# Splitting a 2048-point sequence transform as 128 × 16 with a radix-8 instead of a radix-4 vector stage

## The chip, the cores and the metric

The kernel runs on one core of a Trainium2 chip. The metric is the device time of one execution in microseconds (us). The kernel before took 253.74 us in the median of six runs (253.08 to 256.08).

The engines go by the names the profile gives them: PE multiplies matrices (PEld is its weight load, which overlaps the multiplications), DVE is the vector engine, ACT the scalar engine, POOL and SP here mostly issue DMA transfers. Each engine works through its own instruction list in order.

## The reference, cut to what matters

```python
xn = _layernorm(x, axis=-1)                       # x: 1 x 2048 x 512, bf16
return x + _A_ref(xn, w_r, w_i) + _B_ref(xn, w_gate, w_up, w_down)

def _A_ref(x, w_r, w_i):                          # spectral branch
    X = jnp.fft.rfft2(x.astype(jnp.float32), axes=(-2, -1))
    X = X * (w_r + 1j * w_i)                      # w_r, w_i: 2048 x 257
    return jnp.fft.irfft2(X, s=(S, D), axes=(-2, -1)).astype(jnp.bfloat16)

def _B_ref(x, w_gate, w_up, w_down):              # gated branch
    g = x @ w_gate; u = x @ w_up                  # 512 -> 1792
    return (_gelu(g) * u) @ w_down                # 1792 -> 512
```

S is 2048 (the sequence axis) and D is 512 (the feature axis). A real transform of 512 points has 257 distinct complex outputs, which is where the width of 257 in the kernel comes from.

## The kernel before

Everything is unrolled into straight lists of instructions, one list per engine. A scheduler writes these lists when the kernel is built: of the instructions whose inputs and buffers are free by its own estimate of times, it takes the one with the highest priority. Priority is the order in the program, so the gated branch (lines 265 to 311) comes ahead of the spectral branch; only instructions inside `with hp():` are lifted ahead of everything. Those are matmuls and ACT copies of the spectral branch (lines 327 to 336, 351 to 367 and 431 to 456). The spectral branch's DVE work is not lifted.

**Normalization (lines 232 to 260).** x lies in 16 blocks of 128 rows, where block `b = 8*T + rho` holds the rows `1024*T + 8*tau + rho`. Each block is normalized on DVE, transposed on PE and copied by ACT to `xnT`.

**Gated branch.** There are four chunks of 512 rows, and in each chunk 14 tiles of the hidden axis, 56 tiles in all. For one tile PE runs four `gps` and four `ups` matmuls of 512 columns (lines 271 and 277). ACT and DVE then make the GELU: ACT `sq` and `gsb` from PSUM (283, 285), DVE `wtl` and `z` (287, 292), ACT `sg` (294), DVE `m1` and the product with `ups` into `hT` (296, 297). After the 14 tiles of a chunk, four `dn` accumulations of 14 matmuls each (303) give the branch's output rows; DVE adds x to each and keeps it as `bsp` (310). The tiles `sq`, `gsb`, `wtl`, `z`, `sg` and `m1` come from a pool with two buffers each, so the chain of one tile can overlap that of the next. PSUM has two buffers for `gps`, three for `ups` and one for `dn`.

**Spectral branch, forward.** The feature axis is transformed by matmuls with a cosine and sine matrix `Gt` (`pd`, lines 330 to 335), and ACT copies the result to `Pt`. The sequence axis of 2048 points is then split. With k = 512*m + 128*kc + i, the loop over four `kc` (line 339) loads one 1 MB table `Fkc` and two 257 KB pieces of the spectral weights. For each of four residues r, eight matmuls sum four blocks each against cosine and sine (`cs`, lines 354 and 362). ACT copies them out in four pieces, and DVE combines the halves to `qq` (368, 370). A 4-point transform over r on DVE (`bf`, then `XFk`, lines 373 to 389) gives four values of m, which are multiplied by the complex weights (`tm`, lines 396 to 401).

**Spectral branch, inverse.** After two values of `kc` that belong together (q = kc mod 2), the function `dft8` (line 125) runs an 8-point inverse transform over the eight values of m on DVE and writes `YY`; lines 413 to 421 negate and patch its edges. When both halves q of `YY` are there, 128 `ut` matmuls of 256 columns (line 451) with the 2 MB table `Rt` and 64 `fp` matmuls of 512 columns (468) return to the sequence and feature axes. DVE adds `bsp` (472) and two 1 MB transfers write the output.

Of the kernel before, what the change touches and what calls it, by code (L numbers as in the profile page):

```python
# [12 lines left out]
BF16 = mybir.dt.bfloat16  # L13
ALU = mybir.AluOpType
# [3 lines left out]
D = 512  # L18
DF = 1792
P = 128  # L20
# [4 lines left out]
def _host_constants():  # L25
# [26 lines left out]
    tau = np.arange(P).astype(np.int64)  # L52
    T8 = np.arange(2).astype(np.int64)
    rho8 = np.arange(8).astype(np.int64)
    mp = np.arange(P).astype(np.int64)
    kcv = np.arange(4).astype(np.int64)
    s_val = (1024 * T8[:, None, None] + 8 * tau[None, :, None] + rho8[None, None, :])
    sv = s_val.transpose(1, 0, 2)
    prod = (128 * kcv[:, None, None, None, None] + mp[None, None, None, None, :]) * sv[None, :, :, :, None]
    angF = 2.0 * np.pi * (prod % S) / S  # L60
    Fcos = np.cos(angF).reshape(4, P, 16, P)
    Fsin = np.sin(angF).reshape(4, P, 16, P)
    F = np.stack([Fcos, Fsin], axis=2).reshape(4, P, 2 * 16 * P)
    ii = np.arange(P).astype(np.int64)
    qv = np.arange(2).astype(np.int64)
    tp = np.arange(256).astype(np.int64)
# [6 lines left out]
    bf = ml_dtypes.bfloat16  # L73
# [10 lines left out]
def kernel(  # L84
# [24 lines left out]
    gview = cG.rearrange("(p dt) k -> p dt k", dt=4)  # L109
    giview = cGinv.rearrange("(kt p) d -> p kt d", p=P)  # L110
    rview = cR.rearrange("i (q cs r t) -> i q cs r t", q=2, cs=2, r=8)
    wrv4 = A_w_r.rearrange("(m kc i) k -> i kc m k", m=4, kc=4)
    wiv4 = A_w_i.rearrange("(m kc i) k -> i kc m k", m=4, kc=4)

    tt = nc.vector.tensor_tensor
    HP_OFF = 10_000_000
# [148 lines left out]
    for c in range(4):  # L265
        hT = hpool.tile([P, 14, D], BF16)
        for fc in range(14):
            gps = psA.tile([P, D], FP32)
            ups = psA.tile([P, D], FP32, bufs=3)
            for dt in range(4):  # L270
                nc.tensor.matmul(  # L271
                    gps[:], lhsT=wg[:, dt, fc * P:(fc + 1) * P],
                    rhs=xnT[:, dt, 4 * c:4 * c + 4, :], start=(dt == 0),
                    stop=(dt == 3),
                )
            for dt in range(4):
                nc.tensor.matmul(  # L277
                    ups[:], lhsT=wu[:, dt, fc * P:(fc + 1) * P],
                    rhs=xnT[:, dt, 4 * c:4 * c + 4, :], start=(dt == 0),
                    stop=(dt == 3),  # L280
                )
            sq = mpool.tile([P, D], BF16)
            nc.scalar.activation(out=sq[:], in_=gps[:], func=ACT.Square)  # L283
            gsb = mpool.tile([P, D], BF16)
            nc.scalar.copy(out=gsb[:], in_=gps[:])  # L285
            wtl = mpool.tile([P, D], BF16)
            nc.vector.tensor_scalar(  # L287
                out=wtl[:], in0=sq[:], scalar1=A3, scalar2=C1, op0=ALU.mult,
                op1=ALU.add,
            )  # L290
            z = mpool.tile([P, D], BF16)
            tt(out=z[:], in0=wtl[:], in1=gsb[:], op=ALU.mult)  # L292
            sg = mpool.tile([P, D], BF16)
            nc.scalar.activation(out=sg[:], in_=z[:], func=ACT.Sigmoid, scale=2.0)  # L294
            m1 = mpool.tile([P, D], BF16)
            tt(out=m1[:], in0=sg[:], in1=gsb[:], op=ALU.mult)
            tt(out=hT[:, fc, :], in0=m1[:], in1=ups[:], op=ALU.mult)  # L297
# [19 lines left out]
    with tc.tile_pool(name="p3f", bufs=1) as p3f, tc.tile_pool(  # L317
        name="p3ps", bufs=1, space=bass.MemoryType.PSUM
    ) as p3ps, tc.tile_pool(name="p3g", bufs=1) as p3g, tc.tile_pool(
        name="p3q", bufs=1  # L320
    ) as p3q, tc.tile_pool(name="p3xf", bufs=2) as p3xf, tc.tile_pool(
        name="p3w", bufs=1
    ) as p3w, tc.tile_pool(name="p3cs", bufs=1, space=bass.MemoryType.PSUM) as p3cs:
        Pt = p3f.tile([P, 16, D], BF16)
        blocks4 = [[8 * T8 + r4 + 4 * hi for T8 in range(2) for hi in range(2)]
                   for r4 in range(4)]
        with hp():
            for r4 in range(4):
                for b in blocks4[r4]:
                    pd = p3ps.tile([P, D], FP32)  # L330
                    for dt in range(4):
                        nc.tensor.matmul(  # L332
# [2 lines left out]
                        )  # L335
                    nc.scalar.copy(out=Pt[:, b, :], in_=pd[:])

        XF_by_kc = {}
        for kc in (0, 2, 1, 3):
            Fkc = p3g.tile([P, 2, 16, P], BF16)  # L340
            WRk = p3w.tile([P, 4, 258], BF16)
            WIk = p3w.tile([P, 4, 258], BF16)
            nc.sync.dma_start(
                out=Fkc[:], in_=cF[kc].rearrange("t (c b m) -> t c b m", c=2, b=16)
            )
            nc.sync.dma_start(out=WRk[:, :, 0:257], in_=wrv4[:, kc, :, :])
            nc.sync.dma_start(out=WIk[:, :, 0:257], in_=wiv4[:, kc, :, :])
            qq = p3q.tile([P, 4, 2, 258], BF16)
            for r in range(4):
                cbsb = p3q.tile([P, 2, 256], BF16, tag="cbsb", bufs=1)  # L350
                with hp():
                    cs = p3cs.tile([P, D], FP32, tag="cs")
                    for n, b in enumerate(blocks4[r]):
                        nc.tensor.matmul(  # L354
                            cs[:], lhsT=Fkc[:, 0, b, :], rhs=Pt[:, b, :],
                            start=(n == 0), stop=(n == 3),
                        )
                    nc.scalar.copy(out=qq[:, r, 0, 0:257], in_=cs[:, 0:257])
                    nc.scalar.copy(out=cbsb[:, 0, 0:255], in_=cs[:, 257:512])
                    cs2 = p3cs.tile([P, D], FP32, tag="cs")  # L360
                    for n, b in enumerate(blocks4[r]):
                        nc.tensor.matmul(
                            cs2[:], lhsT=Fkc[:, 1, b, :], rhs=Pt[:, b, :],
                            start=(n == 0), stop=(n == 3),
                        )
                    nc.scalar.copy(out=qq[:, r, 1, 0:257], in_=cs2[:, 0:257])
                    nc.scalar.copy(out=cbsb[:, 1, 0:255], in_=cs2[:, 257:512])
# [1 line left out]
                   in1=cbsb[:, 1, 0:255], op=ALU.subtract)  # L369
                tt(out=qq[:, r, 1, 1:256], in0=qq[:, r, 1, 1:256],  # L370
                   in1=cbsb[:, 0, 0:255], op=ALU.add)
            bf = p3q.tile([P, 2, 4, 258], BF16)
            for p_ in range(2):
                tt(out=bf[:, p_, 0, 0:257], in0=qq[:, 0, p_, 0:257], in1=qq[:, 2, p_, 0:257], op=ALU.add)
                tt(out=bf[:, p_, 1, 0:257], in0=qq[:, 0, p_, 0:257], in1=qq[:, 2, p_, 0:257], op=ALU.subtract)
                tt(out=bf[:, p_, 2, 0:257], in0=qq[:, 1, p_, 0:257], in1=qq[:, 3, p_, 0:257], op=ALU.add)
                tt(out=bf[:, p_, 3, 0:257], in0=qq[:, 1, p_, 0:257], in1=qq[:, 3, p_, 0:257], op=ALU.subtract)
            s02r, d02r, s13r, d13r = (bf[:, 0, k, 0:257] for k in range(4))
            s02i, d02i, s13i, d13i = (bf[:, 1, k, 0:257] for k in range(4))
            XFk = p3xf.tile([P, 4, 2, 258], BF16)  # L380
            XF_by_kc[kc] = XFk
            tt(out=XFk[:, 0, 0, 0:257], in0=s02r, in1=s13r, op=ALU.add)
            tt(out=XFk[:, 0, 1, 0:257], in0=s02i, in1=s13i, op=ALU.add)
            tt(out=XFk[:, 2, 0, 0:257], in0=s02r, in1=s13r, op=ALU.subtract)
            tt(out=XFk[:, 2, 1, 0:257], in0=s02i, in1=s13i, op=ALU.subtract)
            tt(out=XFk[:, 1, 0, 0:257], in0=d02r, in1=d13i, op=ALU.subtract)
            tt(out=XFk[:, 1, 1, 0:257], in0=d02i, in1=d13r, op=ALU.add)
            tt(out=XFk[:, 3, 0, 0:257], in0=d02r, in1=d13i, op=ALU.add)
            tt(out=XFk[:, 3, 1, 0:257], in0=d02i, in1=d13r, op=ALU.subtract)
            for m in range(4):  # L390
                tm = p3w.tile([P, 4, 258], BF16, tag="tm")
                xr_ = XFk[:, m, 0, 0:257]
                xq_ = XFk[:, m, 1, 0:257]
                w_r = WRk[:, m, 0:257]
                w_i = WIk[:, m, 0:257]
                tt(out=tm[:, 0, 0:257], in0=xr_, in1=w_r, op=ALU.mult)
                tt(out=tm[:, 1, 0:257], in0=xq_, in1=w_i, op=ALU.mult)
                tt(out=tm[:, 2, 0:257], in0=xr_, in1=w_i, op=ALU.mult)
                tt(out=tm[:, 3, 0:257], in0=xq_, in1=w_r, op=ALU.mult)
                tt(out=XFk[:, m, 0, 0:257], in0=tm[:, 0, 0:257], in1=tm[:, 1, 0:257], op=ALU.add)  # L400
                tt(out=XFk[:, m, 1, 0:257], in0=tm[:, 2, 0:257], in1=tm[:, 3, 0:257], op=ALU.subtract)
            if kc >= 2:
                q = kc - 2
                Xe, Xo = XF_by_kc[q], XF_by_kc[kc]
                ins = []
                for m8 in range(8):
                    src = Xe if m8 % 2 == 0 else Xo
                    m4 = m8 // 2
                    ins.append((src[:, m4, 0, 0:257], src[:, m4, 1, 0:257]))
                outs_ = [(YY[:, q, rp, 0, 0:257], YY[:, q, rp, 1, 0:257]) for rp in range(8)]  # L410
                dft8(ins, outs_, SC)
                for rp in range(8):
                    nc.vector.tensor_scalar(
                        out=YY[:, q, rp, 2, 0:257], in0=YY[:, q, rp, 1, 0:257],
                        scalar1=-1.0, scalar2=None, op0=ALU.mult,
                    )
                    nc.vector.tensor_copy(
                        out=YY[:, q, rp, 1, 256:257], in_=YY[:, q, rp, 0, 256:257]
                    )
                    nc.vector.tensor_copy(  # L420
                        out=YY[:, q, rp, 0, 256:257], in_=YY[:, q, rp, 2, 256:257]
                    )

    p3ut = ctx.enter_context(tc.tile_pool(name="p3ut", bufs=1))
    UT = p3ut.tile([P, 8, 4, 256], BF16)
# [78 lines left out]
```

## Time and profile before

| | us |
|---|---|
| median of six runs | 253.74 |
| the profiled execution, its own time | 254.92 |
| its span from first to last instruction | 253.1 |
| PE busy in it | 230.5 (91%) |
| DVE busy in it | 191.0 (75%) |
| ACT busy in it | 143.3 (57%) |

The mean granted PE clock is 0.993 of full speed. Two habits of the profile matter. The recorded duration of a matmul is longer than the distance between the starts of two matmuls in a row[...]: 128x512 matmuls are recorded with some 380 ns, but four of them take 0.86 us on the chain of work that ended last. DVE records overlap in the same way. What a stage can carry is therefore read from the distance of starts, and a busy share tells only whether something was in flight.

### The profile page before, as it was taken

What the parts mean: (1) busy time and instruction counts of PE and PEld (TensorE: products, weight loads), DVE (VectorE), ACT (ScalarE), POOL (GpSimd) and SP (SyncE); (2) the same over time, 40 slices, a digit from 0 to 9 for tenths busy, and PEclk for the clock granted to TensorE, in tenths of its full rate; (3) what the DMA queues carried; (4) which work ended last, traced back from release to release, by engine and by line L of the source; (5) the groups of instructions that cost most, each with busy time, mean ns of one, the idle gap of its engine ahead of it and who ended that gap; (6) DMA issues with size and microseconds to landing.
All of it is one profiled execution on the core that took longest, in us unless ns stands there. A gap on an engine that the chain in (4) does not pass through costs nothing.

```text
span 253.1 us, 3506 instructions
## 1 busy us (share of the span) xinstructions
PE 230.5 (91%) x1120; PEld 107.4 (42%) x1120; DVE 191.0 (75%) x661; ACT 143.3 (57%) x302; POOL 11.6 (5%) x20
## 2 busy tenths in 40 slices
PE   0398999999999989999999999999899999999990
PEld 0254444444444334444444443444344467644440
DVE  2997664346999989999946999999899970144571
ACT  2279987768753328986334888830269987600000
POOL 8530000000000000000000000000000000000000
PEclk9999999999999999999999999999999999999997
DMA  6999920001303503000105021009100000000044
GB/s 222 350 348 372 326 84 1 0 3 23 142 22 103 187 18 88 1 3 0 38 26 186 4 45 38 0 7 351 39 21 0 5 0 0 3 0 0 0 166 166
DMA packets 9954, 21.45 MB, mean 85 GB/s; under 512 B 785, under 2 KB 7057, under 8 KB 9041
## 3 DMA queue, kind: packets, MB, share of 16 engines
q1 hardware_dynamic: 8112, 13.12, 15.9%
q0 software_dynamic: 1824, 8.13, 9.1%
q8 instruction: 8, 0.13, 0.2%
q14 instruction: 10, 0.07, 0.1%
HBM read 19.14 MB, written 2.10 MB: 84 GB/s over the span
## 4 chain that ended last, share of the span: by engine, by line
PE 55%; DVE 24%; ACT 8%; DMA 8%; issue 3%; DVEq 0%; POOLq 0%; ACTq 0%
PE ups L277 11%; PE gps L271 10%; PE dn L303 9%; PE ut L451 6%; PE fp L468 6%; DVE hT L297 5%; PE cs L354 4%; PE pd L332 4%; DMA Rt<-cR 3%; DVE z L292 3%; DMA Fkc<-cF 2%; ACT sg L294 2%; DVE stats L242 2%; DMA xt<-in_A_x_dram 2%; ACT sq L283 2%
## 5 line engine op out<-in xcount | busy, mean ns | idle before, releaser
L271 PE MATMUL gps<-xnT,wg 128*128 128x512 bf16 x224 | 61.6, 383 | 0.1
L277 PE MATMUL ups<-xnT,wu 128*128 128x512 bf16 x224 | 61.2, 381 | 0.2 <-DVE hT L297 0.2
L303 PE MATMUL dn<-wd,hT 128*128 128x512 bf16 x224 | 53.5, 379 | 0.9 <-DVE hT L297 0.6
L283 ACT ACTIVATE sq<-gps 128x512 bf16<-128x512 f32 x56 | 33.3, 595 | 26.9 <-PE gps L271 26.5
L294 ACT ACTIVATE sg<-z 128x512 bf16<-128x512 bf16 x56 | 35.3, 632 | 15.1 <-DVE z L292 14.1
L303 PEld LDWEIGHTS <-hT 128*128 128x128 bf16 x224 | 21.8, 97 | 29.5 <-issue 2.6
L277 PEld LDWEIGHTS <-wu 128*128 128x128 bf16 x224 | 22.0, 98 | 26.4 <-issue 2.4
L285 ACT CAST gsb<-gps 128x512 bf16<-128x512 f32 x56 | 32.7, 584 | 0.0
L271 PEld LDWEIGHTS <-wg 128*128 128x128 bf16 x224 | 22.0, 99 | 24.8 <-issue 0.7
L287 DVE TENSOR_SCALAR wtl<-sq 128x512 bf16<-128x512 bf16 x56 | 16.1, 288 | 19.6 <-ACT sq L283 19.5
L292 DVE TENSOR_TENSOR z<-wtl,gsb 128x512 bf16<-128x512 bf16 x56 | 23.5, 420 | 2.5 <-ACT gsb L285 2.3
L354 PE MATMUL cs<-Pt,Fkc 128*128 128x512 bf16 x64 | 18.4, 378 | 1.4 <-DMA Fkc<-cF 1.2
L310 DVE TENSOR_TENSOR bsp<-xblk,dn 128x512 bf16<-128x512 bf16 x16 | 10.9, 684 | 10.8 <-PE dn L303 10.8
L451 PE MATMUL ut<-Rt,YY 128*128 128x256 bf16 x128 | 17.1, 271 | 1.8 <-DMA Rt<-cR 1.1
L257 PE MATMUL tp<-ident,xn 128*128 128x128 bf16 x64 | 7.9, 263 | 11.6 <-DVE xn L251 10.6
L332 PE MATMUL pd<-Gt,xnT 128*128 128x512 bf16 x64 | 16.4, 379 | 0.0
L451 PEld LDWEIGHTS <-YY 128*128 128x128 bf16 x128 | 12.1, 97 | 8.0 <-issue 3.0
L468 PE MATMUL fp<-Ginv,UT 128*128 128x512 bf16 x64 | 14.9, 378 | 0.0
L456 ACT CAST UT<-ut 128x256 bf16<-128x256 f32 x32 | 11.6, 375 | 3.7 <-PE ut L451 3.0
L472 DVE TENSOR_TENSOR osb<-bsp,fp 128x512 bf16<-128x512 bf16 x16 | 11.0, 688 | 3.3 <-PE fp L468 3.3
L242 DVE BATCH_NORM_STATS2 stats<-xt 128x6 f32<-128x512 bf16 x16 | 10.4, 663 | 4.0 <-DMA xt<-in_A_x_dram 4.0
L257 PEld LDWEIGHTS <-xn 128*128 128x128 bf16 x64 | 5.9, 128 | 15.0 <-DVE xn L251 11.3
(222 smaller groups left out, 263.5 us busy)
## 6 DMA issues: line engine op xcount, KB each, us to landing
Fkc<-cF SPq DMA_DIRECT2D x4, 1024.0 KB, 5.5
xt<-in_A_x_dram SPq DMA_DIRECT2D x4, 512.0 KB, 6.1
xblk<-in_A_x_dram SPq DMA_DIRECT2D x16, 128.0 KB, 2.6
Rt<-cR POOLq DMA_DIRECT2D x1, 2048.0 KB, 8.8
out_dram<-osb SPq DMA_DIRECT2D x2, 1024.0 KB, 3.9
wd<-in_B_w_down_dram POOLq DMA_DIRECT2D x2, 896.0 KB, 15.9
wg<-in_B_w_gate_dram POOLq DMA_DIRECT2D x4, 384.0 KB, 16.3
wu<-in_B_w_up_dram POOLq DMA_DIRECT2D x4, 384.0 KB, 16.2
```

The costliest lines, as they stand in the source:

```text
L271: nc.tensor.matmul(gps[:], lhsT=wg[:, dt, fc * P:(fc + 1) * P], rhs=xnT[:, dt, 4 * c:4 * c + 4, :], start=(dt == 0), stop=(dt == 3),)
L277: nc.tensor.matmul(ups[:], lhsT=wu[:, dt, fc * P:(fc + 1) * P], rhs=xnT[:, dt, 4 * c:4 * c + 4, :], start=(dt == 0), stop=(dt == 3),)
L283: nc.scalar.activation(out=sq[:], in_=gps[:], func=ACT.Square)
L285: nc.scalar.copy(out=gsb[:], in_=gps[:])
L287: nc.vector.tensor_scalar(out=wtl[:], in0=sq[:], scalar1=A3, scalar2=C1, op0=ALU.mult, op1=ALU.add,)
L292: tt(out=z[:], in0=wtl[:], in1=gsb[:], op=ALU.mult)
L294: nc.scalar.activation(out=sg[:], in_=z[:], func=ACT.Sigmoid, scale=2.0)
L303: nc.tensor.matmul(dn[:], lhsT=hT[:, fc, r * P:(r + 1) * P], rhs=wd[:, fc, :], start=(fc == 0), stop=(fc == 13),)
L332: nc.tensor.matmul(pd[:], lhsT=xnT[:, dt, b, :], rhs=Gt[:, dt, :], start=(dt == 0), stop=(dt == 3),)
L354: nc.tensor.matmul(cs[:], lhsT=Fkc[:, 0, b, :], rhs=Pt[:, b, :], start=(n == 0), stop=(n == 3),)
L451: nc.tensor.matmul(ut[:], lhsT=lt, rhs=rh, start=(q == 0 and pi_ == 0), stop=(q == 1 and pi_ == 1),)
L468: nc.tensor.matmul(fp[:], lhsT=UT[:, rp, t, aT * P:(aT + 1) * P], rhs=Ginv[:, t, :], start=(t == 0), stop=(t == 3),)
```

## The change

The sequence transform is split as 2 halves q times 8 values of m: k = 256*m + 128*q + i. Each half now loads one 1 MB table `Fq` and two 514 KB pieces of the weights, so two tables are loaded in place of four. For each of eight residues r, four matmuls sum two blocks each. The 4-point transform over r becomes an 8-point one, done by a first call of `dft8` into `XFq`; after the weights a second call of `dft8`, the one there was, writes `YY`. The order of the `pd` blocks follows the new residues. `qq`, `XFq` and the weight tiles have eight slots in place of four, `bf` is gone, the pool of `XFq` has one buffer in place of two, and the gated branch's `wtl`, `z` and `sg` have one buffer each in place of two.

```diff
-            wtl = mpool.tile([P, D], BF16)
+            wtl = mpool.tile([P, D], BF16, bufs=1)
...
-            z = mpool.tile([P, D], BF16)
+            z = mpool.tile([P, D], BF16, bufs=1)
...
-            sg = mpool.tile([P, D], BF16)
+            sg = mpool.tile([P, D], BF16, bufs=1)
...
-    ) as p3q, tc.tile_pool(name="p3xf", bufs=2) as p3xf, tc.tile_pool(
+    ) as p3q, tc.tile_pool(name="p3xf", bufs=1) as p3xf, tc.tile_pool(
...
-        for kc in (0, 2, 1, 3):
-            Fkc = p3g.tile([P, 2, 16, P], BF16)
-            WRk = p3w.tile([P, 4, 258], BF16)
-            WIk = p3w.tile([P, 4, 258], BF16)
+        for q in range(2):
+            Fq = p3g.tile([P, 2, 16, P], BF16)
+            WRq = p3w.tile([P, 8, 258], BF16)
+            WIq = p3w.tile([P, 8, 258], BF16)
...
-            for r in range(4):
+            for r in range(8):
...
-                    for n, b in enumerate(blocks4[r]):
+                    for T8 in range(2):
+                        b = 8 * T8 + r
                         nc.tensor.matmul(
-                            cs[:], lhsT=Fkc[:, 0, b, :], rhs=Pt[:, b, :],
-                            start=(n == 0), stop=(n == 3),
+                            cs[:], lhsT=Fq[:, 0, b, :], rhs=Pt[:, b, :],
+                            start=(T8 == 0), stop=(T8 == 1),
                         )
...
-            bf = p3q.tile([P, 2, 4, 258], BF16)
-            for p_ in range(2):
-                tt(out=bf[:, p_, 0, 0:257], in0=qq[:, 0, p_, 0:257], in1=qq[:, 2, p_, 0:257], op=ALU.add)
...
-            tt(out=XFk[:, 3, 1, 0:257], in0=d02i, in1=d13r, op=ALU.subtract)
-            for m in range(4):
+            XFq = p3xf.tile([P, 8, 2, 258], BF16)
+            dft8(
+                [(qq[:, n, 0, 0:257], qq[:, n, 1, 0:257]) for n in range(8)],
+                [(XFq[:, m, 0, 0:257], XFq[:, m, 1, 0:257]) for m in range(8)],
+                SC,
+            )
+            for m in range(8):
...
+            dft8(
+                [(XFq[:, m, 0, 0:257], XFq[:, m, 1, 0:257]) for m in range(8)],
+                [(YY[:, q, rp, 0, 0:257], YY[:, q, rp, 1, 0:257]) for rp in range(8)],
+                SC,
+            )
```

More of the change, by code (lines that the diff above doesn't have):

```diff
@@ L54, in _host_constants @@
     rho8 = np.arange(8).astype(np.int64)
-    mp = np.arange(P).astype(np.int64)
-    kcv = np.arange(4).astype(np.int64)
+    iv0 = np.arange(P).astype(np.int64)
+    qv0 = np.arange(2).astype(np.int64)
     s_val = (1024 * T8[:, None, None] + 8 * tau[None, :, None] + rho8[None, None, :])
     sv = s_val.transpose(1, 0, 2)
-    prod = (128 * kcv[:, None, None, None, None] + mp[None, None, None, None, :]) * sv[None, :, :, :, None]
+    prod = (128 * qv0[:, None, None, None, None] + iv0[None, None, None, None, :]) * sv[None, :, :, :, None]
     angF = 2.0 * np.pi * (prod % S) / S
-    Fcos = np.cos(angF).reshape(4, P, 16, P)
-    Fsin = np.sin(angF).reshape(4, P, 16, P)
-    F = np.stack([Fcos, Fsin], axis=2).reshape(4, P, 2 * 16 * P)
+    Fcos = np.cos(angF).reshape(2, P, 16, P)
+    Fsin = np.sin(angF).reshape(2, P, 16, P)
+    F = np.stack([Fcos, Fsin], axis=2).reshape(2, P, 2 * 16 * P)
     ii = np.arange(P).astype(np.int64)
@@ L111 @@
     rview = cR.rearrange("i (q cs r t) -> i q cs r t", q=2, cs=2, r=8)
-    wrv4 = A_w_r.rearrange("(m kc i) k -> i kc m k", m=4, kc=4)
-    wiv4 = A_w_i.rearrange("(m kc i) k -> i kc m k", m=4, kc=4)
+    wrv = A_w_r.rearrange("(m q i) k -> i q m k", m=8, q=2)
+    wiv = A_w_i.rearrange("(m q i) k -> i q m k", m=8, q=2)
     tt = nc.vector.tensor_tensor
@@ L324 @@
         Pt = p3f.tile([P, 16, D], BF16)
-        blocks4 = [[8 * T8 + r4 + 4 * hi for T8 in range(2) for hi in range(2)]
-                   for r4 in range(4)]
         with hp():
-            for r4 in range(4):
-                for b in blocks4[r4]:
+            for r8 in range(8):
+                for T8 in range(2):
+                    b = 8 * T8 + r8
                     pd = p3ps.tile([P, D], FP32)
@@ L336 @@
                     nc.scalar.copy(out=Pt[:, b, :], in_=pd[:])
-        XF_by_kc = {}
-        for kc in (0, 2, 1, 3):
-            Fkc = p3g.tile([P, 2, 16, P], BF16)
-            WRk = p3w.tile([P, 4, 258], BF16)
-            WIk = p3w.tile([P, 4, 258], BF16)
+        for q in range(2):
+            Fq = p3g.tile([P, 2, 16, P], BF16)
+            WRq = p3w.tile([P, 8, 258], BF16)
+            WIq = p3w.tile([P, 8, 258], BF16)
             nc.sync.dma_start(
-                out=Fkc[:], in_=cF[kc].rearrange("t (c b m) -> t c b m", c=2, b=16)
+                out=Fq[:], in_=cF[q].rearrange("t (c b m) -> t c b m", c=2, b=16)
             )
-            nc.sync.dma_start(out=WRk[:, :, 0:257], in_=wrv4[:, kc, :, :])
-            nc.sync.dma_start(out=WIk[:, :, 0:257], in_=wiv4[:, kc, :, :])
-            qq = p3q.tile([P, 4, 2, 258], BF16)
-            for r in range(4):
+            nc.sync.dma_start(out=WRq[:, :, 0:257], in_=wrv[:, q, :, :])
+            nc.sync.dma_start(out=WIq[:, :, 0:257], in_=wiv[:, q, :, :])
+            qq = p3q.tile([P, 8, 2, 258], BF16)
+            for r in range(8):
                 cbsb = p3q.tile([P, 2, 256], BF16, tag="cbsb", bufs=1)
@@ L352 @@
                     cs = p3cs.tile([P, D], FP32, tag="cs")
-                    for n, b in enumerate(blocks4[r]):
+                    for T8 in range(2):
+                        b = 8 * T8 + r
                         nc.tensor.matmul(
-                            cs[:], lhsT=Fkc[:, 0, b, :], rhs=Pt[:, b, :],
-                            start=(n == 0), stop=(n == 3),
+                            cs[:], lhsT=Fq[:, 0, b, :], rhs=Pt[:, b, :],
+                            start=(T8 == 0), stop=(T8 == 1),
                         )
@@ L360 @@
                     cs2 = p3cs.tile([P, D], FP32, tag="cs")
-                    for n, b in enumerate(blocks4[r]):
+                    for T8 in range(2):
+                        b = 8 * T8 + r
                         nc.tensor.matmul(
-                            cs2[:], lhsT=Fkc[:, 1, b, :], rhs=Pt[:, b, :],
-                            start=(n == 0), stop=(n == 3),
+                            cs2[:], lhsT=Fq[:, 1, b, :], rhs=Pt[:, b, :],
+                            start=(T8 == 0), stop=(T8 == 1),
                         )
@@ L371 @@
                    in1=cbsb[:, 0, 0:255], op=ALU.add)
-            bf = p3q.tile([P, 2, 4, 258], BF16)
-            for p_ in range(2):
-                tt(out=bf[:, p_, 0, 0:257], in0=qq[:, 0, p_, 0:257], in1=qq[:, 2, p_, 0:257], op=ALU.add)
[L375 to L388, printed above, removed]
-            tt(out=XFk[:, 3, 1, 0:257], in0=d02i, in1=d13r, op=ALU.subtract)
-            for m in range(4):
+            XFq = p3xf.tile([P, 8, 2, 258], BF16)
[5 more added lines that the diff above has]
+            for m in range(8):
                 tm = p3w.tile([P, 4, 258], BF16, tag="tm")
[L392 to L395, printed above, removed]
+                xr_ = XFq[:, m, 0, 0:257]
+                xq_ = XFq[:, m, 1, 0:257]
+                w_r = WRq[:, m, 0:257]
+                w_i = WIq[:, m, 0:257]
                 tt(out=tm[:, 0, 0:257], in0=xr_, in1=w_r, op=ALU.mult)
@@ L399 @@
                 tt(out=tm[:, 3, 0:257], in0=xq_, in1=w_r, op=ALU.mult)
[L400 to L422, printed above, removed]
+                tt(out=XFq[:, m, 0, 0:257], in0=tm[:, 0, 0:257], in1=tm[:, 1, 0:257], op=ALU.add)
+                tt(out=XFq[:, m, 1, 0:257], in0=tm[:, 2, 0:257], in1=tm[:, 3, 0:257], op=ALU.subtract)
+            dft8(
[3 more added lines that the diff above has]
+            )
+            for rp in range(8):
+                nc.vector.tensor_scalar(
+                    out=YY[:, q, rp, 2, 0:257], in0=YY[:, q, rp, 1, 0:257],
+                    scalar1=-1.0, scalar2=None, op0=ALU.mult,
+                )
+                nc.vector.tensor_copy(
+                    out=YY[:, q, rp, 1, 256:257], in_=YY[:, q, rp, 0, 256:257]
+                )
+                nc.vector.tensor_copy(
+                    out=YY[:, q, rp, 0, 256:257], in_=YY[:, q, rp, 2, 256:257]
+                )
     p3ut = ctx.enter_context(tc.tile_pool(name="p3ut", bufs=1))
```

## The prediction

> **What bounds the kernel now.** I read the page's busy table and its 40 slices first.
>
> ```profile
> PE 230.5 (91%) x1120; PEld 107.4 (42%) x1120; DVE 191.0 (75%) x661; ACT 143.3 (57%) x302; POOL 11.6 (5%) x20
> ...
> PE   0398999999999989999999999999899999999990
> ...
> DVE  2997664346999989999946999999899970144571
> ```
>
> PE looks like the bound. But DVE, 75% on the mean, shows 9s from about 60 to 200 us, so there are two bounds in that stretch. The answer by windows makes this exact; I cut at 60 us and at 206.5 us, where DVE issues the last operation on YY.
>
> ```profile
> core 0: us, PE busy (x) PEld busy (x) DVE busy (x) ACT busy (x) POOL busy (x), PEclk, DMA share, GB/s
> 15.00:60.00 45.00, 43.97 (x220) 20.40 (x219) 26.49 (x74) 36.10 (x74) 1.34 (x2) 1.00 0.43 141
> 60.00:206.50 146.50, 141.82 (x657) 63.02 (x655) 137.68 (x533) 91.02 (x194) 0.55 (x1) 1.00 0.18 58
> 206.50:253.10 46.60, 40.57 (x222) 21.20 (x220) 16.60 (x26) 10.78 (x28) 0.00 (x0) 0.96 0.11 45
> ```
>
> In the middle stretch DVE has something in flight for 137.7 of 146.5 us: whatever is added to it there moves the moment when YY is complete. I call that moment T. What follows T is the tail, from the timeline:
>
> ```profile
> 206.22 0.28 DVE L420 COPY YY<-YY 128x1 bf16<-128x1 bf16 x2
> ...
> 206.69 12.22 PE L451 MATMUL ut<-Rt,YY 128*128 128x256 bf16 x92
> 218.75 1.03 PE L271 MATMUL gps<-xnT,wg 128*128 128x512 bf16 x4
> 219.61 1.03 PE L277 MATMUL ups<-xnT,wu 128*128 128x512 bf16 x4
> 220.47 3.29 PE L303 MATMUL dn<-wd,hT 128*128 128x512 bf16 x14
> ```
>
> After T come the rest of ut, one gated tile (1.7 us), all four dn of the last chunk (12.4 us, from 3.1 each on the chain) and fp; all of it is PE work. The last fp ends at 247.4, and the last add and the output transfer take 5.7 more.
>
> Third, the timeline of a stretch dense with gated tiles, for the real price of a DVE operation and for the use of the double buffers.
>
> ```profile
> 98.65 0.29 DVE L123 TENSOR_TENSOR SC<-SC 128x257 bf16<-128x257 bf16 x1
> 98.85 0.42 DVE L292 TENSOR_TENSOR z<-wtl,gsb 128x512 bf16<-128x512 bf16 x1
> ...
> 99.52 1.36 ACT L294 ACTIVATE sg<-z 128x512 bf16<-128x512 bf16 x2
> ...
> 99.79 0.42 DVE L292 TENSOR_TENSOR z<-wtl,gsb 128x512 bf16<-128x512 bf16 x1
> ...
> 100.33 0.42 DVE L296 TENSOR_TENSOR m_756<-sg,gsb 128x512 bf16<-128x512 bf16 x1
> ```
>
> The 257-wide operation is recorded with 0.29 us, but its successor starts 0.20 us later. Starts in a row elsewhere give 0.203 for it, 0.135 for a 257-wide negation, 0.065 for a one-column copy, and 0.20, 0.335, 0.335 and 0.60 for wtl, z, m1 and hT: 1.47 us of DVE a tile; bsp is 0.60. This list can be tested: 45 tiles (66.2), 12 bsp (7.2) and the spectral operations after 60 us (65.4 of them in all, less some 2.0 before) make 136.8 us, against 137.7 measured. So DVE is costed by starts.
>
> **The change, part by part.**
>
> *PE, removed.* 4 kc x 4 r x 8 = 128 cs matmuls become 2 x 8 x 4 = 64. By 0.216 us each (0.86 for four on the chain) that is 13.8 us. The first half q has 32, as kc = 0 had, beside the same 64 pd, so nothing is gained before 60 us; the gain lies in the middle stretch. The waits for F shrink too, by 1.2 us at 89 us, where PE stood for the second table.
>
> *DVE, added.* bf and XFk go: 4 x 16 = 64 operations. Two more dft8 come, each of 52 two-operand operations and 4 scalings: 104 and 8. Net 40 x 0.203 + 8 x 0.135 = 9.2 us. Here a rule speaks against my price. The Trainium skill, "VectorE: DVE Perf Modes", section "The DRAIN you can't avoid", says that the next operation does not start until the pipe is empty (and that one not held starts earlier). By full recorded durations the sum would be 40 x 0.291 + 8 x 0.224 = 13.4 us. The rows show the next start inside the recorded duration, and the ledger closes to 1 us with starts, so I take 9.2.
>
> *ACT.* 64 copies out of cs before, 64 after; but 32 fall in the first half instead of 16 in kc = 0. Their starts are about 0.28 apart, so 4.5 us more come on ACT between 28 and 62, where it is busy some 75% of the time. This may delay a gated tile or so (1.5 us of DVE later); against it the even half of the first dft8 can start before 60, in DVE's idle time there (up to 12 operations, 2.4 us). I count -1 us for both; bounds -2.4 and +2.
>
> *Waits in the middle.* DVE's 8.7 us of idleness there are nearly all listed in its timeline. 5.5 of them lie at 127 to 135 us, when it had no spectral work and waited for cs, dn and ACT:
>
> ```profile
> 130.10 0.69 DVE L310 TENSOR_TENSOR bsp<-xblk,dn 128x512 bf16<-128x512 bf16 x1 [1.65 <-PE dn L303]
> ...
> 134.93 0.29 DVE L370 TENSOR_TENSOR qq<-qq,cbsb 128x255 bf16<-128x255 bf16 x1 [2.15 <-ACT qq L366]
> ```
>
> With two long halves, cs of q = 1 can run as soon as the first dft8 of q = 0 has read qq, with q = 0's weights and second dft8 still to be done. So filling is at hand throughout and I take back 5.5 us.
>
> *DMA.* Two tables and 2 MB fewer. The weight transfers are doubled in size; those of q = 1 wait in SP's queue for the last product of q = 0, with xblk loads behind them, which have four buffers. XFq's single buffer orders only DVE against itself. Both at nothing; the cover is the gated work and DVE's backlog, and without it a late pair would cost its 3 us landing.
>
> *Single buffers.* Above, the second z (99.79) starts while the first sg runs, and the second sg starts about 100.2, before m1 (100.33) has read the first. With one buffer z of the next tile waits for sg, and sg for m1. ACT's next sq and gsb stand behind a waiting sg, and PE's gps behind those. An isolated tile near the end (z at 220.98, m1 at 222.10) gives 1.12 us from z to m1; with m1's 0.335 the loop is 1.46 us, under PE's 1.73 a tile. If hT (0.60) and one filling operation (0.20) get between m1 and z, it is 2.26. The rule to "double-buffer for performance" (Trainium Kernel Development and Optimization, "Best Practices") is about DMA with compute; taken for this chain it would price 46 tiles after 60 us at 0.53 each, 24 us. No row of this trace shows single buffers. I take the end near 1.46, as either order of m1 and z makes progress and DVE has other work to fill the wait, plus 1.5 us of new small waits; the bounds are 0 and 24.
>
> *Sum.* With PE ahead, the last tile (1.5) and four bsp (2.4) also fall before T. T = 206.5 + 9.2 + 1.5 + 2.4 - 5.5 - 1.0 + 1.5 = 214.6. The tail then holds ut and fp alone: ut begins some 1.8 us before T (the edge operations of the first rp come first), 128 x 0.130 = 16.7, fp 64 x 0.216 = 13.8, 0.4 between, and 5.7: T + 34.8 = 249.4 in span. By PE alone the gated tiles' matmuls would be through at about 60 + 46 x 1.73 + 36 (three chunks' dn) + 7 (cs of q = 1) + 5 of small gaps = 188, so PE has room. The span falls by 3.7; outside the span lie 1.8 us (254.9 against 253.1), kept. The profiled execution would take 251.2 and the median, 1.2 under it, 250.0.
>
> **Rivals.**
>
> *PE alone is the bound* (full gain). 13.8 + 1.2 less: 238.7. For: nearly every slice of PE is a 9. Against: DVE's middle stretch has only 8.7 us idle for 9.2 added. Chance 0.12, with cases to 244.
>
> *The middle moves as I say but the pieces cancel*: no idleness regained (5.5) makes 255.5; half of it, 252.8. The gain in matmuls buys only idle PE time. Chance 0.22 for within 1%.
>
> *Slower: the gated chain goes in step.* Place: z, sg, m1 with one buffer each. Price: the loop per tile. The last tile's PE work moves from 188 by 46 x (P - 1.73); from P = 2.0 (12 us) the last dn slip behind T, and ut, which is lifted, goes ahead of them. At 2.26 (24 us) the tiles end at 212, and dn 12.4, ut 16.7, fp 13.8 and 5.7 follow: 261 in span, about 261 in the median. For: the trace shows both second buffers in use. Against: the loop can close at 1.46. Chance 0.24.
>
> **How the numbers follow.** My forecast has 0.42 (246 to 251), full gain 0.12, same 0.22, slower 0.24. About 1% is what a measurement of this kernel can tell from no change, so: faster 0.54, same 0.22, slower 0.24. The range of 242 to 260 leaves out the best end of the first rival and the worst of the last.
>
> **What would show it.** cs matmuls 64; DVE some 9 us more by starts; DVE without a long gap from 60 to the end of YY at about 213 to 216; the last dn before most of ut, and a last stretch of ut and fp alone. PE idle before T by 10 us or more. The forecast is wrong if YY ends after 220, if dn stands behind ut again, or if z and sg wait on each other with DVE idle in each tile.

## The result and the profile after

The changed kernel took 250.81 us in the median of ten runs; the kernel before, run beside it on the same chip as well, 254.71 in the median of twenty. The ratio is 0.9852 with a 95% interval of 0.9818 to 0.9887: 1.5% faster, some 3.8 us. The forecast had 250.0 and a fall of 3.7. The profiled execution took 249.52 with a span of 247.8.

The page of the changed kernel, its busy table and slices:

```profile
PE 219.1 (88%) x1056; PEld 101.7 (41%) x1056; DVE 199.2 (80%) x709; ACT 142.0 (57%) x302; POOL 11.6 (5%) x20
...
PE   0298999999999999999999999999999683999990
...
DVE  2998664558999999999999889999999999000771
PEclk9999999999999999999999999999999999799997
```

PE has 64 matmuls fewer and for the first time a hole, the 6 8 3 from about 192 to 211 us. DVE has 48 operations more and shows 9s up to the end of that hole. The granted PE clock has a dip just behind it. The windows, cut at 60 us and now at 211.5, just after DVE's last operation on YY (it starts at 211.0):

```profile
core 0: us, PE busy (x) PEld busy (x) DVE busy (x) ACT busy (x) POOL busy (x), PEclk, DMA share, GB/s
...
60.00:211.50 151.50, 141.56 (x637) 61.49 (x635) 148.90 (x577) 87.16 (x177) 0.55 (x1) 1.00 0.12 39
211.50:247.80 36.30, 29.90 (x177) 17.25 (x174) 11.01 (x16) 10.79 (x29) 0.00 (x0) 0.92 0.14 58
```

DVE is busy for 148.9 of 151.5 us between 60 us and T. It was 137.7 of 146.5: 11.2 us more work and 6.2 us less idleness. What follows T has shrunk from 46.6 to 36.3 us. The timeline of PE around T says why:

```profile
187.52 1.03 PE L277 MATMUL ups<-xnT,wu 128*128 128x512 bf16 x4
188.38 3.03 PE L303 MATMUL dn<-wd,hT 128*128 128x512 bf16 x13
192.41 0.39 PE L303 MATMUL dn<-wd,hT 128*128 128x512 bf16 x1 [0.99 <-DVE hT L297]
...
202.13 3.18 PE L303 MATMUL dn<-wd,hT 128*128 128x512 bf16 x14 [1.08 <-DVE bsp L310]
205.73 0.39 PE L434 MATMUL ut<-Rt,YY 128*128 128x256 bf16 x2 [0.42 <-DVE YY L120]
209.11 0.39 PE L434 MATMUL ut<-Rt,YY 128*128 128x256 bf16 x2 [2.99 <-DVE YY L396]
209.85 17.14 PE L434 MATMUL ut<-Rt,YY 128*128 128x256 bf16 x120 [0.35 <-ACT UT L439]
227.45 14.56 PE L451 MATMUL fp<-Ginv,UT 128*128 128x512 bf16 x64 [0.46 <-ACT UT L439]
```

The last gated tile leaves PE at 188.5 us, all dn are done before ut, and PE then waits for DVE, which still works at YY. The number in brackets is PE's idle time before the row and what ended it: these are all DVE, and the longest is for the last edges of YY.

### The profile page after: what moved, and what is told of

It is laid out like the page before. It is cut to its first block, busy times and chain, and to the rows that moved or that the text cites. A ratio compares the mean times of both kernels' runs of the same rounds, so it can differ in the third digit from the quotient of the medians.

```text
span 247.8 us, 3409 instructions
## 1 busy us (share of the span) xinstructions
PE 219.1 (88%) x1056; PEld 101.7 (41%) x1056; DVE 199.2 (80%) x709; ACT 142.0 (57%) x302; POOL 11.6 (5%) x20
## 3 DMA queue, kind: packets, MB, share of 16 engines
q1 hardware_dynamic: 7760, 11.02, 13.8%
## 4 chain that ended last, share of the span: by engine, by line
PE 40%; DVE 39%; ACT 7%; issue 6%; DMA 5%; POOLq 0%; DVEq 0%; ACTq 0%
PE gps L271 8%; PE ups L277 8%; PE ut L434 7%; PE fp L451 6%; DVE hT L297 5%; PE pd L331 5%; DVE SC L123 4%; DVE SC L120 3%; DMA Rt<-cR 3%; DVE wtl L287 3%; DVE bsp L310 3%; DVE z L292 3%; PE cs L353 2%; DVE stats L242 2%; DVE YY L120 2%
## 5 line engine op out<-in xcount | busy, mean ns | idle before, releaser
L277 PE MATMUL ups<-xnT,wu 128*128 128x512 bf16 x224 | 60.2, 379 | 0.1
L303 PE MATMUL dn<-wd,hT 128*128 128x512 bf16 x224 | 52.9, 379 | 5.1 <-DVE bsp L310 3.6
L434 PE MATMUL ut<-Rt,YY 128*128 128x256 bf16 x128 | 18.4, 289 | 4.3 <-DVE YY L396 3.0
L257 PE MATMUL tp<-ident,xn 128*128 128x128 bf16 x64 | 7.3, 257 | 12.0 <-DVE xn L251 10.7
L331 PE MATMUL pd<-Gt,xnT 128*128 128x512 bf16 x64 | 17.4, 378 | 0.0
L434 PEld LDWEIGHTS <-YY 128*128 128x128 bf16 x128 | 12.9, 103 | 10.2 <-DVE YY L396 3.3
L335 ACT CAST Pt<-pd 128x512 bf16<-128x512 f32 x16 | 9.4, 586 | 4.9 <-PE pd L331 4.9
```

Source lines behind the costliest of these rows:

```text
L277: nc.tensor.matmul(ups[:], lhsT=wu[:, dt, fc * P:(fc + 1) * P], rhs=xnT[:, dt, 4 * c:4 * c + 4, :], start=(dt == 0), stop=(dt == 3),)
L303: nc.tensor.matmul(dn[:], lhsT=hT[:, fc, r * P:(r + 1) * P], rhs=wd[:, fc, :], start=(fc == 0), stop=(fc == 13),)
L331: nc.tensor.matmul(pd[:], lhsT=xnT[:, dt, b, :], rhs=Gt[:, dt, :], start=(dt == 0), stop=(dt == 3),)
L434: nc.tensor.matmul(ut[:], lhsT=lt, rhs=rh, start=(q == 0 and pi_ == 0), stop=(q == 1 and pi_ == 1),)
```

## The experiments

Three questions: what each part of the change is worth alone, what bounds each kernel, and whether the change leaves something on the table. Differences in us are worked out as the ratio's distance from 1 times 255 us. T is read from the start of the last DVE operation on YY in each profile. Each edit makes the scheduler write new lists, so a difference holds the new order as well as the work that was added or taken, and one of a microsecond or two is not a pure cost.

### Each part alone

**The matmuls alone.** The kernel before, summing two of four blocks in each cs; two of the four blocks are left out of the computation, and nothing else is changed.

```diff
-                    for n, b in enumerate(blocks4[r]):
+                    for n, b in enumerate(blocks4[r][2:4]):
...
-                            start=(n == 0), stop=(n == 3),
+                            start=(n == 0), stop=(n == 1),
```

> The PE part of the change alone: the kernel before with 64 of its 128 cs matmuls left out (two of four blocks are not summed), 13.8 us less PE work, DVE's work and the buffers as they were. My theory: the last tile and the last dn move ahead of T, T itself moves to 207 to 210, and the tail of 34.8 us follows: -8 to -11 us. Rival (PE alone is the bound of the kernel before): -13 to -14 us. Rival (it is hidden anyway): 0 to -2 us.

Measured: 242.17 us, ratio 0.947 [0.942, 0.952], 13.5 us less. That is the whole of the 13.8 us removed, and my figure of 8 to 11 is missed: the rival that had PE alone as the bound of the kernel before was right. T is at 201.3, some 5 us earlier than before, though DVE has the same operations. Its windows:

```profile
60.00:201.50 141.50, 135.07 (x608) 59.39 (x618) 139.06 (x534) 87.59 (x186) 0.55 (x1) 1.00 0.19 60
201.50:240.30 38.80, 32.62 (x193) 18.52 (x192) 12.38 (x18) 10.54 (x29) 0.00 (x0) 0.98 0.13 54
```

DVE is busy for 139.1 of 141.5 us: its 8.8 us of idleness before T in the kernel before are down to 2.4. Those gaps were waits for PE, directly (bsp for dn) or through ACT (qq for cs); none of either is left in this run's timeline. PE in turn now waits 2.3 us for DVE ahead of ut, so this kernel stands about where the two bounds meet.

**The DVE operations alone.** The kernel before with three of six products for each m done twice, 48 operations:

```diff
                 tt(out=tm[:, 3, 0:257], in0=xq_, in1=w_r, op=ALU.mult)
+                tt(out=tm[:, 1, 0:257], in0=xq_, in1=w_i, op=ALU.mult)
+                tt(out=tm[:, 2, 0:257], in0=xr_, in1=w_i, op=ALU.mult)
+                tt(out=tm[:, 3, 0:257], in0=xq_, in1=w_r, op=ALU.mult)
```

> The DVE part alone: the kernel before with 48 of its products done a second time, 48 x 0.203 = 9.7 us more DVE work, PE's work and the buffers as they were. If DVE is simply on the path: +8 to +10 us. My theory: T moves by 7 to 10 us, but PE, which is full until then, uses the time for the tile and part of the dn that stand in the tail: +1 to +6 us.

Measured: 261.76 us, ratio 1.023 [1.018, 1.028], 5.8 us more, at the upper end of what I expected. So DVE was near enough to being the bound that more work showed, but not one for one. T moved by 17.3 us (206.3 to 223.6), not by the 7 to 10 expected: DVE is busy 14.4 us more between 60 us and T, 9.7 for the doubled products and the rest mostly for the last tile and for bsp operations that now come before T, and it waits 3 us longer, with one gap of 2.90 us behind a wait of PE for the table `Rt`. What follows T shrank from 46.6 to 36.3 us, as in the changed kernel.

**The single buffers alone.** The kernel before with `bufs=1` for wtl, z and sg.

> The kernel before with one buffer in place of two for wtl, z and sg, and nothing else of the change. My theory: the chain closes, as the profile of the changed kernel shows m1 and the next z back to back and 1.67 to 1.88 us a tile against PE's 1.73, so 0 to +2 us. Rival (the chain of tiles goes in step and costs the change much of its gain): +6 to +24 us.

Measured: 256.24 us, ratio 1.0053 [1.0026, 1.0080], 1.4 us more. The rival of a chain in step is out at this load. The changed kernel's DVE rows in a dense stretch show how the chain closes:

```profile
93.27 0.41 DVE L296 TENSOR_TENSOR m_779<-sg,gsb 128x512 bf16<-128x512 bf16 x1
93.60 0.41 DVE L292 TENSOR_TENSOR z<-wtl,gsb 128x512 bf16<-128x512 bf16 x1
...
94.94 0.41 DVE L296 TENSOR_TENSOR m_802<-sg,gsb 128x512 bf16<-128x512 bf16 x1
95.27 0.41 DVE L292 TENSOR_TENSOR z<-wtl,gsb 128x512 bf16<-128x512 bf16 x1
...
96.82 0.41 DVE L296 TENSOR_TENSOR m_825<-sg,gsb 128x512 bf16<-128x512 bf16 x1
```

The next z stands right behind m1, ahead of hT, and a tile takes 1.67 and 1.88 us, on the mean 1.78 against PE's 1.73.

The three parts add up to -13.5 + 5.8 + 1.4 = -6.3 us, 2.5 more than the change brought. The order in which they are taken matters. Without the matmuls DVE has hardly a gap left, and then its added work seems to count fully: T moves from 201.3 there to 211.0 in the changed kernel, 9.7 us for 9.2 of work. This was not tested apart, since these two kernels differ in buffers and tables as well.

### What bounds the changed kernel

**Less PE work.** One of the two blocks in each cs is left out of the computation, 32 matmuls.

```diff
-                    for T8 in range(2):
+                    for T8 in range(1, 2):
...
-                            start=(T8 == 0), stop=(T8 == 1),
+                            start=True, stop=True,
```

> The changed kernel with 32 of its 64 cs matmuls left out (the blocks of the first 1024 rows are not summed), 32 x 0.216 = 6.9 us less PE work ahead of T. My theory (DVE sets T, PE stands idle before it): 0 to -1 us. Rival (PE still bounds the middle): -5 to -7 us.

Measured: 249.60 us, ratio 0.980 [0.975, 0.986] to the kernel before, against 0.985 for the changed kernel: 1.2 us less for 6.9 removed, with intervals that overlap. The rest became idle time: ahead of ut PE waits 7.53 and 2.17 us for DVE in place of 0.42 and 2.99.

**Less DVE work.** Two of the four products for each m are left out of the computation, 32 operations; the last sum reads the first two.

```diff
-                tt(out=tm[:, 2, 0:257], in0=xr_, in1=w_i, op=ALU.mult)
-                tt(out=tm[:, 3, 0:257], in0=xq_, in1=w_r, op=ALU.mult)
...
-                tt(out=XFq[:, m, 1, 0:257], in0=tm[:, 2, 0:257], in1=tm[:, 3, 0:257], op=ALU.subtract)
+                tt(out=XFq[:, m, 1, 0:257], in0=tm[:, 0, 0:257], in1=tm[:, 1, 0:257], op=ALU.subtract)
```

> The changed kernel with 32 of the 96 spectral products left out (two of the four for each m), 32 x 0.203 = 6.5 us less DVE work. My theory: -5 to -6.5 us, as T moves ahead by what DVE no longer does and PE has about 8 us of idle time before T to give. Rival (PE bounds): 0 to -1 us.

Measured: 243.94 us, ratio 0.959 [0.954, 0.964], 6.7 us less than the changed kernel for 6.5 removed; T moves from 211.0 to 205.0. That the two figures agree so well is in part chance: the PE clock does not fall here, which makes ut 1.3 us shorter, and ten dn matmuls, 2.2 us, now come behind ut. The change has moved the kernel from one bound to the other: before, PE's work counted one for one, and now DVE's does.

### The second buffers again

**Products through SC, and two buffers for z and sg.** The room comes from the tile of the products, so a control has the products in SC and keeps the single buffers.

```diff
-            z = mpool.tile([P, D], BF16, bufs=1)
+            z = mpool.tile([P, D], BF16)
...
-            sg = mpool.tile([P, D], BF16, bufs=1)
+            sg = mpool.tile([P, D], BF16)
...
-                tm = p3w.tile([P, 4, 258], BF16, tag="tm")
+                tm = SC[:, 2 * (m % 4):2 * (m % 4) + 2].rearrange("p a b c -> p (a b) c")
```

> The changed kernel with two buffers again for z and sg; the room comes from the products, which go to SC in place of a tile of their own. My theory (single buffers cost nothing where DVE has filling work): -0.5 to +1 us. Rival (the chain in step delays the changed kernel): -2 to -6 us.

> The changed kernel with its products in SC and the single buffers left as they are: the kernel with two buffers again, less its second buffers. In that one DVE stood 3.4 us for cs of the second half at 150 to 157 us, as its other work had run out, and PE's clock fell to half at 212 to 219. If this order comes from the products' place or from chance in the order, this kernel is as slow (ratio 0.995 to 1.003 to the kernel before). If the second buffers themselves bring it (tiles run further ahead, spectral work is pushed back), it is as fast as the changed kernel (0.982 to 0.989).

Measured: with two buffers 255.19 us, ratio 0.999 [0.996, 1.002]; the control with single ones 250.51, ratio 0.985 [0.980, 0.990]. Giving the buffers back made the kernel 3.7 us slower, which neither side of the first expectation had. The control is as fast as the changed kernel, so the loss comes with the second buffers and not with the place of the products. DVE's timeline in the slower one has waits for the second half's cs:

```profile
151.07 0.29 DVE L370 TENSOR_TENSOR qq<-qq,cbsb 128x255 bf16<-128x255 bf16 x1 [0.64 <-ACT qq L366]
153.74 0.29 DVE L370 TENSOR_TENSOR qq<-qq,cbsb 128x255 bf16<-128x255 bf16 x1 [0.69 <-ACT qq L366]
156.40 0.29 DVE L370 TENSOR_TENSOR qq<-qq,cbsb 128x255 bf16<-128x255 bf16 x1 [2.09 <-ACT qq L366]
```

The listed gaps of DVE between 60 us and T sum to 6.1 us here and 2.7 in the control, and T is at 216.8 against 211.8. So most of the loss, 3.4 of 5.0 us, is DVE waiting with no other work. Why the scheduler's order comes out worse with more buffers the runs don't show: by 140 us DVE has finished 37 tiles in both. That is left open.

### The late second half

In the changed kernel cs of q = 1 runs at 68 and 82 us for r = 0 and 1 and at 133 to 150 for the rest. The buffer of cbsb is single, and the DVE corrections that free it have low priority, behind all of q = 0. Lifting them:

```diff
-                tt(out=qq[:, r, 0, 1:256], in0=qq[:, r, 0, 1:256],
+                with hp():
+                    tt(out=qq[:, r, 0, 1:256], in0=qq[:, r, 0, 1:256],
...
```

> The changed kernel with the two corrections of qq on DVE lifted to the priority of cs. In the changed kernel cs of the second half ran for r = 0 and 1 at 68 and 82 us and for the rest at 133 to 150, behind corrections of low priority. Lifted, they should run by about 100 us and the gaps of DVE at 137 to 148 (1.2 us) close. My theory (DVE's total is the bound): 0 to -2 us, as there is little idle time to win. Rival (the late second half costs the changed kernel its gain): -3 to -6 us.

> The kernel before with the corrections of qq lifted to the priority of cs, the step that took 4 us from the changed kernel. If PE bounds the kernel before, as leaving out half of its cs matmuls showed (13.5 us for 13.8 removed), closing DVE's gaps at 127 to 135 us wins little: 0 to -2 us. If DVE's gaps were on its path as in the changed kernel: -3 to -5 us.

Measured, lifted in the changed kernel: 246.97 us, ratio 0.968 [0.964, 0.973], 4.4 us less than the changed kernel. That lies in the rival's range and not in mine: the late second half did cost the changed kernel part of its gain. cs of q = 1 now ends at 88 us, and DVE's idle time between 60 us and T falls from 2.6 to 1.1 us. The span fell from 247.8 to 244.3. T gives 2.1 of these 3.5 us (211.0 to 208.9) and the rest is the PE clock: the long run of 120 ut takes 15.83 us in place of 17.14.

Measured, lifted in the kernel before: 253.94 us, ratio 0.999 [0.996, 1.003]. Here T is at 183.2 us, 23 us earlier than before, and the time is the same:

```profile
182.02 15.83 PE L452 MATMUL ut<-Rt,YY 128*128 128x256 bf16 x120
183.16 0.16 DVE L421 COPY YY<-YY 128x1 bf16<-128x1 bf16 x1
...
218.63 1.03 PE L277 MATMUL ups<-xnT,wu 128*128 128x512 bf16 x4
```

PE takes ut early and the gated tiles late, and the last tile leaves it at 219.7 us, where it left at 220.6 before. So an earlier T gains nothing in the kernel before, whose PE has the same work to do in either order.

### A version that beats both

The same arithmetic in fewer, wider operations: real and imaginary parts, and two to eight slots or four values of m, in one instruction.

```diff
-            cadd(s02r, e[0][0], e[2][0])
-            cadd(s02i, e[0][1], e[2][1])
...
+            cadd(V(h, 4, 2), X[:, h:4:2], X[:, h + 4:8:2])
...
-            for m in range(8):
...
+            for m in range(0, 8, 4):
+                xr_ = XFq[:, m:m + 4, 0, 0:257]
...
+                tt(out=pr_[0], in0=xr_, in1=w_r, op=ALU.mult)
```

> The changed kernel with the same arithmetic in fewer and wider DVE operations: real and imaginary parts, and 2 to 8 slots, in one instruction where the operation is the same; the products for 4 values of m go through SC. At 0.07 us of fixed cost for each operation saved (0.203 for 257 columns, 0.335 for 512) DVE has some 15 us less: dft8 11.1 to 9.3 four times, products 19.5 to 14.4, edges of YY 4.2 to 1.4. My theory: T moves from 211 to about 198, until PE is the bound at about 238 to 241 us of span: 7 to 10 us less than the changed kernel, about 241 us in the median. Rival (PE bounds already): 0 to -2 us.

> The kernel before with its spectral DVE operations merged in the same way, some 13 us less of DVE work; matmuls and buffers of the gated branch as they were. My theory: PE bounds this kernel once DVE is lighter, and its work is unchanged: -1 to -5 us. Rival (DVE alone is the bound): -10 to -13 us.

> The merged version with the corrections of qq lifted as well. The merged version left DVE idle for 5.6 us at 122 to 135 us, waiting for cs of the second half and for ACT. My theory: T moves ahead by 2 to 4 us and the median comes to 240.5 to 242.5 us; below that PE is the bound. If the gaps only move elsewhere: 0 to -1 us.

Measured: the changed kernel merged 244.32 us, ratio 0.960 [0.955, 0.964], 6.5 us less than the changed kernel. That is short of the 7 to 10 expected. DVE's busy time fell by 13.0 us instead of 15 (199.2 to 186.2), and T came only to 202.3 instead of 198 as DVE waited for the late second half: its idle time between 60 us and T grew from 2.6 to 6.8 us. (Of this 4.3 us lie at 122 to 135 us; the 5.6 in the third expectation above is too high.) The kernel before merged in the same way: 253.87, ratio 0.993 [0.990, 0.997], 1.7 us less. Lightening DVE is worth some four times as much after the change as before it.

Merged and lifted: 242.49 us, ratio 0.947 [0.943, 0.952], 9.7 us less than the changed kernel and at the slow end of what I expected. T moved by 8.0 us, not by 2 to 4. The PE timeline from just before T to the end:

```profile
192.71 0.39 PE L289 MATMUL dn<-wd,hT 128*128 128x512 bf16 x1 [0.99 <-DVE hT L283]
193.66 0.39 PE L408 MATMUL ut<-Rt,YY 128*128 128x256 bf16 x2 [0.55 <-DVE YY L375]
194.40 17.13 PE L408 MATMUL ut<-Rt,YY 128*128 128x256 bf16 x120 [0.35 <-ACT UT L413]
...
222.30 12.70 PE L425 MATMUL fp<-Ginv,UT 128*128 128x512 bf16 x56
```

YY is complete at 194.5 us, and from then on PE has work without a break, three dn among it. PE is the main bound again: T came 8.0 us earlier than without the lifting, but the span is only 1.7 us shorter (240.7 against 242.4). Some DVE cost is left all the same. Just ahead of ut PE waits 1.9 us, and the 120 ut take 17.13 us where they take 15.83 at full clock. The span is close to that of the kernel before with half its cs matmuls left out (240.3), which has as many matmuls.

## Why the prediction was right, and where it was not

**The main claim held**: PE's gain is spent on DVE's added work, T moves less than DVE gains as its idle time is used up, and the dn move ahead of T.

- *DVE by starts.* The middle stretch was to hold 137.7 + 9.2 + 1.5 + 2.4 - 1.0 = 149.8 us of DVE work; it holds 148.9. By recorded durations it would have been 154.0. More of DVE's work than forecast came early: its busy time between 15 and 60 us grew by 2.7 us, against the 1.0 taken.
- *Idle time regained.* 5.5 back and 1.5 of new waits had been counted, 4.7 us left; 2.6 were left. T was forecast at 214.6 and came at 211.0.
- *Its reason was wrong.* "cs of q = 1 can run as soon as the first dft8 of q = 0 has read qq" overlooked the wait for cbsb, whose readers are low-priority DVE operations. cs ran 50 us later than that sentence says; the gap did not open because DVE's backlog lasted just long enough. In the version with second buffers it did not.
- *The tail.* ut and fp alone were to take 34.8 us after T; it was 36.8. PE stood nearly still for 3.7 us before ut, the clock fell, and the 120 ut took 17.14 us, 1.3 more than at full clock.
- *PE's room.* The tiles' last matmuls were put at about 188 us and ended at 188.5. PE was to be idle for 10 us or more before T; between 190 and 210 it is 7.7.
- *Single buffers at 1.5 us*: alone they cost 1.4, a tile at 1.78 us and not 2.26. The 24 us that double-buffering as a rule would have priced did not appear, and two buffers were even slower here.
- *What cancelled.* T came 3.6 us earlier than forecast and the tail was 2.0 us longer, so the span of 247.8 is only 1.6 under the 249.4 forecast. The median was to lie 1.2 us under the profiled execution and lay 1.3 above it. That 250.0 and 250.81 are so close is in part luck, though the mechanism held.

**Where the reading of the kernel before was wrong.** "Whatever is added to it there moves the moment when YY is complete": added work did move T, by 17.3 us with the products doubled. But the prediction also started from T as the moment that carries the end, and for the kernel before this is not so: T moved ahead by 23 us there with no gain, and 13.8 us of PE work taken away gave 13.5. PE was the bound of the kernel before, and DVE's 9s were for the most part work that PE's pace left room for. The sum came out right since it was made for the changed kernel, where T does carry the end. The rivals of full gain and of a chain in step fell: the first because DVE becomes the bound on the way, the second by the tile's 1.78 us. The rival of no change within 1% fell too, if not by much: it had half or none of DVE's idle time regained, and 6.2 of 8.8 us were.

## What to carry to other kernels

Two engines that both show 9s are told apart by taking work from each in turn: 13.8 us off PE gave 13.5 before the change, 6.9 off PE gave 1.2 and 6.5 off DVE 6.7 after it. Work traded from the bound to its neighbour pays only until the neighbour becomes the bound, and from there the next step is to lighten the neighbour, which had been worth little before (1.7 us) and was then worth 6.5. Where a helper operation of low priority frees a single buffer, the high priority of what waits for it is void.

## What the hardware showed unasked

In several runs the PE clock fell to half when PE had little or nothing to do for some microseconds, and it came back only some time after PE was loaded again. Windows of the changed kernel with less PE work, where PE has no matmul from 198 to 205 us:

```profile
196.00:198.00 2.00, 1.94 (x9) 1.00 0.00 0
...
202.00:204.00 2.00, 0.00 (x0) 0.77 0.00 0
204.00:206.00 2.00, 0.53 (x2) 0.50 0.00 0
...
212.00:214.00 2.00, 1.98 (x13) 0.67 0.03 8
214.00:216.00 2.00, 1.98 (x16) 1.00 0.00 0
```

The column after the count of matmuls is the granted clock. It falls some 5 us after the last matmul and is back some 4 us after ut began in earnest, at 209.1. In the changed kernel the same happens at 210 to 214 us with a mean clock of 0.57; the first 24 ut of its long run take 4.46 us where 24 take 3.1 later.

The fall can come sooner. In the kernel before with more DVE work PE waits 2.45 us for the table `Rt`, and the clock is at half when it starts again:

```profile
188.00:189.00 1.00, 0.98 (x5) 1.00 1.07 459
189.00:190.00 1.00, 0.00 (x0) 1.00 0.24 98
190.00:191.00 1.00, 0.00 (x0) 1.00 0.04 16
191.00:192.00 1.00, 0.57 (x3) 0.73 0.00 0
```

In the merged and lifted kernel it falls at 195.0 us, after 3.3 us in which PE ran fewer than ten matmuls and no gap was longer than 0.99 us. The Trainium skill, "TensorE: Matmul & The Clock Gate", Part 1, describes such a gate, half clock after an idle window of about 3.4 us and full clock after as much sustained work. The return agrees with it to within a microsecond. The fall in these last two runs came after less idle time than that, and what exactly sets it off stays open. So a wait that ends just ahead of a stage full of matmuls costs more than itself, 1.3 us in the changed kernel, and part of what lifting the corrections gained was this. No run here tested it by filling the gap.
